# A two-layer attention kernel on one core: in the token tail, the read-out of every odd tile moved up into the round of the even tile before it

## The chip, the core and the metric

The kernel runs on one core of a Trainium2 chip. The metric is the device time of one execution in microseconds, a median over runs. Engines are named as in the profile: PE (TensorE matmuls), PEld (its weight loads), DVE (VectorE), ACT (ScalarE), POOL (GpSimd), SP (the queue that issues most DMAs).

## What is computed

The model has four blocks, A, B, A, B, each with a residual and a layer norm in front. S = 2048 tokens, D = 576 features, 32 heads of 18. A is softmax attention with one shared key and value head; B is linear attention with a feature map of two softmaxes. Cut to what matters here:

```python
# B, per head
phi_q = concat(softmax(q @ w_phi), softmax(-(q @ w_phi)))     # 36 features
kv    = einsum("sf,sd->fd", phi_k, v);  z = phi_k.sum(s)
o     = (phi_q @ kv) / (phi_q @ z + 1e-6)                     # the "read-out"
x     = x + concat_heads(o) @ wo
```

The kernel calls one A and the B behind it a layer, so it has two layers.

## The kernel before, in words

Tokens are worked in 16 tiles of 128. A layer first runs the attention of A (`attend`), with the keys and features of B mixed in. When the last tile's state is known (`leave`, `finish_state`), the state of B stands in `kvb`, and the features of every query tile in DRAM (`phi`). Then comes the tail, on which this case turns. It takes one token tile after another through these steps:

- `load_features` (L718 and L719 on SP): the tile's features from DRAM into `pht`. There are two such buffers, one for even tiles and one for odd ones (`room`).
- the read-out (`read_out`, first part): 22 small matmuls at L826 (the profile records two instructions for each of them, 44 in all) multiply `pht` by `kvb` into two banks of PSUM; each matmul writes only 64 of the output rows, so it uses half of the array's columns. For each bank DVE adds epsilon to the denominators (L833), inverts them (L834) and multiplies (L835); a copy (L836) completes `xo`.
- the transposes (`transposed`): four matmuls at L308 and one at L312 turn `xo` (128 tokens by 640) into two banks. ACT copies the first bank to `xs3` as the high part (L132) and the second (L314), DVE subtracts to get the low part (L135, L317).
- the projection (`project`, L258): 28 matmuls, 14 for each half of the output, with the high and low parts of the weights `wob` (tiles `wahi`, `walo` in this stage). The first two products of a half read the high part of `xs3` alone, the third the low part. DVE adds the result to the residual (L322), and SP stores the tile (L1646 in the last layer, L1648 in the first).
- in the first layer the tail goes on into the next attention (`next_queries`): layer norm of the finished tile (L284 to L291 on DVE, L289 on POOL, L298 and L299 on ACT, into `xn`), five transposes of `xn`, and, for every second tile, the query projection (`project_queries`): 70 matmuls at L465, whose results DVE splits (L494, L498), and a smaller part a round later (L515, L520).

The order is written by generators. Each step ends in `yield STAGE`; `pipelined` starts one tile a round and takes every active tile, the oldest first, to its next `STAGE`; what `project_queries` adds stands last in a round. So a round holds the projection of one tile, the transposes of the next and the read-out of the one after that. A read-out is two rounds after its load, the transposes one round after the read-out, the projection one round after that. What the program writes is then ordered for each engine by the framework's scheduler, which may put a step earlier where it expects a wait. PSUM has seven banks in this stage, given out in turn; `xo` and `xs3` have two buffers each.

Of the kernel before, what the change touches and what calls it, by code (L numbers as in the profile page):

```python
# [52 lines left out]
STAGE = None  # L53
# [9 lines left out]
def kernel(ctx, tc, x_in, wq, wk, wv, wo, wqkv, w_phi, wob, out):  # L63
# [168 lines left out]
    def reload_w4(pool):  # L232
        room_w4(pool)
        for half in range(2):
            nc.sync.dma_start(w4[half].bitcast(F32).rearrange("p k c -> p (k c)"), w4d[half])
# [19 lines left out]
    def project(dst, w, c0, xs, after=None, products=range(len(PRODUCTS)), last=LASTP):  # L255
        for j, n in enumerate(products):
            slot, half, k = PRODUCTS[n]
            T.matmul(dst, xs[:, slot, :], w[half][:, k, c0 : c0 + HALF],  # L258
                     start=(n == 0), stop=(n == last))
            if n == last:  # L260
                if after is not None:
                    after()
                yield -250
            elif j % 2:
                yield 250
# [4 lines left out]
    def bankful(kind, ps, shape=(P, HALF)):  # L270
        yield Kind(kind)
        return ps.tile(list(shape), F32, name="ps")
# [21 lines left out]
    def layer_norm(i, stats, pool, E, tag="xn"):  # L294
        rstd, bias = stats[i]
        xn = pool.tile([P, 5 * P], F32, name=tag)
        if E is A:
            A.activation(xn[:, :D], xres[i], AF.Identity, scale=rstd, bias=bias)  # L298
            A.activation(xn[:, D:], xn[:, 512:D], AF.Copy)  # L299
        else:  # L300
            V.tensor_scalar(xn[:, :D], xres[i], rstd, bias, op0=ALU.mult, op1=ALU.add)
            V.tensor_copy(xn[:, D:], xn[:, 512:D])
        return xn

    def transposed(xn, xs, ps, hi_engine, lo_engine=V):
        pa = ps.tile([P, 4, P], F32, name="ps")
        for k in range(4):
            T.transpose(pa[:, k, :], xn[:, k * P : (k + 1) * P], idf)  # L308
        split(xs[:, 0:4, :], xs[:, 5:9, :], pa, hi_engine, lo_engine)
        yield -440  # L310
        pb = ps.tile([P, P], F32, name="ps")
        T.transpose(pb, xn[:, 512:], idf)  # L312
        if hi_engine is A:
            A.activation(xs[:, 4, :], pb, AF.Copy)  # L314
        else:
            V.tensor_copy(xs[:, 4, :], pb)
        lo_engine.tensor_sub(xs[64:P, 4, :], pb[64:P, :], xs[64:P, 4, :].bitcast(F32))  # L317
        yield -110

    def add_residual(i, b, po):  # L320
        xr = xres[i][:, b * HALF : (b + 1) * HALF]
        V.tensor_add(xr, xr, po)  # L322
# [458 lines left out]
    def advance(job, count=1):  # L781
        while count:
            v = next(job, DONE)
            if v is DONE:
                return
            count -= v is not STAGE and not isinstance(v, Kind) and v < 0
# [31 lines left out]
    def read_out(i, pht, st, sp, ps):  # L818
        xo = sp.tile([P, 5 * P], F32, name="xo")
        xv = xo[:, :D].rearrange("p (h d) -> p h d", d=DH)  # L820
        for g0, g1 in ((0, 8), (8, NKG)):
            pn = ps.tile([P, 8 * NW], F32, name="ps")
            for g in range(g0, g1):
                hs = KG if g < NKG - 1 else 2
                for t0 in (0, 64):
                    T.matmul(pn[t0 : t0 + 64, (g - g0) * NW : (g - g0) * NW + hs * (DH + 1)],  # L826
                             pht[: 2 * DH * hs, g, t0 : t0 + 64],
                             st["kvb"][: 2 * DH * hs, g, : hs * (DH + 1)], start=True, stop=True)
            h0, h1 = g0 * KG, min(g1 * KG, H)
            nv = pn[:, : (h1 - h0) * (DH + 1)].rearrange("p (h e) -> p h e", e=DH + 1)  # L830
            den = small.tile([P, 24], F32, name="den")
            dv = den[:, : h1 - h0]
            V.tensor_scalar(dv, nv[:, :, DH], 1e-6, None, op0=ALU.add)  # L833
            V.reciprocal(dv, dv)  # L834
            V.tensor_mul(xv[:, h0:h1, :], nv[:, :, :DH], dv[:, :, None].to_broadcast([P, h1 - h0, DH]))  # L835
        V.tensor_copy(xo[:, D:], xo[:, 512:D])  # L836
        yield STAGE
        xs = sp.tile([P, 9, P], F32R, name="xs3")
        yield from transposed(xo, xs, ps, A)
        yield STAGE  # L840
        for b in range(2):
            po = yield from bankful("P", ps)
            yield from project(po, st["wob"], b * HALF, xs, lambda: add_residual(i, b, po))
# [544 lines left out]
    for layer in range(LAYERS):  # L1388
        last = layer == LAYERS - 1
        st.update(start_state(bw), added=set(), loaded=set())  # L1390
        with tc.tile_pool(name="a1o", bufs=2) as a1o:
# [166 lines left out]
            def feature_room(name):  # L1558
                return bw.tile([P, H, 2, DH], F32, name=name)
# [26 lines left out]
        with psx, tc.tile_pool(name=f"s{layer + 1}", bufs=2) as sp:  # L1586
            if not last:
                reload_w4(sp)

            def leave():  # L1590
                xn = layer_norm(c, stats, sp, A, "xo")
                advance(second_keys)
                xl = sp.tile([P, 9, P], F32R, name="xs3")
                advance(transposed(xn, xl, ps, A, LOE), 2)
                queued = [queries_in(i, x, feature_room(name), st, ps, spills[layer])
                          for i, x, name in ((KEPT, kept, "featk"), (c - 1, xs, "featq"))]
                advance(queued[0])
                both = sp.tile([P, 9, PW], F32R, name="xsc").bitcast(F32).rearrange("p a b -> p (a b)")
                ek, eq = (both[:, k * 2 * D : (k + 1) * 2 * D].rearrange("p (h s d) -> p h s d", s=2, d=DH)
                          for k in range(2))  # L1600
                last_keys = keys_in(c, xl, ek, st, ps)
                queued.append(queries_in(c, xl, eq, st, ps, spills[layer]))
                advance(last_keys, 2)
                run(load("wob", "a", wob, slice(0, D), engines=(A, V)))
                advance(last_keys, 2)
                if not last:
                    run(load("wq", "b", wq, slice(0, D), engines=(A, G)))
                advance(queued[0])
                advance(last_keys)
                advance(queued[2])  # L1610
                run(finish_state(st, sp, ps))
                advance(queued[2])
                advance(queued[1])
                run(queued[0])
                before = None
                for i in traced(nc)[mark:]:
                    if i.engine == mybir.EngineType.PE:
                        if before is not None:
                            tc.add_manual_dep(i, before, NOSYNC, reason="order")
                        before = i.name  # L1620
                return queued[1:]

            def flips(queued):
                for rounds, job, count in ((1, 0, 1), (3, 0, 3), (2, 1, 3)):
                    for _ in range(rounds):
                        yield STAGE
                    advance(queued[job], count)
                for job in queued:
                    run(job)

            def room(i):
                if i % 2:
                    return sp.tile([P, NKG, P], F32, name="pht", bufs=1)
                return bw.tile([P, NKG, P], F32, name="pht")

            def token_tile(i):
                pht = room(i)
                load_features(pht, spills[layer], i)
                if i not in left:
                    xres[i] = sp.tile([P, D], F32, name="xt", bufs=6)  # L1640
                    nc.sync.dma_start(xres[i], xd[i])
                yield STAGE
                yield STAGE
                yield from read_out(i, pht, st, sp, ps)
                if last:
                    nc.sync.dma_start(out[i * P : (i + 1) * P, :], xres[i])  # L1646
                else:
                    nc.sync.dma_start(xd[i], xres[i])  # L1648
                    yield STAGE
                    yield from next_queries(i, None, layer + 1, st, bw, sp, ps)  # L1650

            order = range(NT)
            st["sp"] = sp
            jobs = [token_tile(i) for i in order]
            for job in jobs[:2]:
                next(job)
            st["late"].append(flips(leave()))
            if last:
                run(pipelined(jobs, st["late"]))
            else:  # L1660
                settle(layer + 1, ps, jobs)
# [27 lines left out]
```

## Time and profile before

| | us |
|---|---|
| median of 3 runs | 2626.08 |
| lowest and highest run | 2624.30, 2628.52 |
| span of the profiled execution (first to last instruction) | 2624.6 |
| first layer's tail, first to last read-out | 1230.2 to 1375.6 |
| second layer's tail, first read-out to the end | 2519.5 to 2624.6 |

The span is that of one profiled execution; the page gives no time for it beside the span, which lies within the three runs, 1.5 us under their median. Over the span PE is busy 99%, ACT 82%, DVE 48%. In a timeline row the columns are start and duration in us, engine, line, operation, tiles (out<-in), shapes and the number of instructions merged, and in brackets how long the engine sat idle before and what ended that.

### The profile page before, as it was taken

Reading aid. Unit: us, or ns where it says so; the run is one execution under the profiler, and the core shown is the slowest. Engines: PE = TensorE matmul, PEld = TensorE weight load, DVE = VectorE, ACT = ScalarE, POOL = GpSimd, SP = SyncE. Lnnn points to the kernel's source line nnn. Section 1 sums busy time; section 2 is a strip of 40 time slices with the busy share of each in tenths; the row PEclk is TensorE's granted clock in tenths of the full one; section 3 lists DMA queues with packets and bytes.
Section 4 is the critical chain, followed back from the end, with each engine's and each line's share of the span. In section 5 each row is a group of like instructions: output and inputs, shape, how many; then the busy total and the mean of one; then the engine's idle time right before and its main releaser. Section 6 shows DMA issues by size and latency. Waiting matters only on the chain. (4 is left out here: it accounts for less than half of the span.)

```text
span 2624.6 us, 55489 instructions
## 1 busy us (share of the span) xinstructions
PE 2585.7 (99%) x22002; PEld 1428.7 (54%) x22002; DVE 1252.3 (48%) x2831; ACT 2163.5 (82%) x2578; POOL 66.0 (3%) x106
## 2 busy tenths in 40 slices
PE   7999999999999999999999999999999999999999
PEld 7634444444444444438996344444444444444598
DVE  7434554444444444427775324444444444444265
ACT  5699899999999999993335999999999999999721
POOL 1000000000000000002000000000000000000010
PEclk9999999999999999999999999999999999999999
DMA  6456352222222222225644222222222222222164
GB/s 194 139 137 185 97 153 59 59 60 57 58 57 61 61 61 61 61 53 179 196 138 131 82 57 57 59 61 56 61 61 61 61 61 61 61 60 57 38 197 145
DMA packets 491632, 232.94 MB, mean 89 GB/s; under 512 B 237734, under 2 KB 458214, under 8 KB 491366
## 3 DMA queue, kind: packets, MB, share of 16 engines
q1 hardware_dynamic: 490326, 227.26, 31.5%
q8 instruction: 175, 2.87, 0.5%
q10 hardware_dynamic: 1040, 2.06, 0.3%
q14 instruction: 91, 0.75, 0.1%
HBM read 130.62 MB, written 96.67 MB: 87 GB/s over the span
## 5 line engine op out<-in xcount | busy, mean ns | idle before, releaser
L1101 ACT ACTIVATE pt<-sc 128x1024 f32<-128x1024 f32 x2032 | 1923.4, 1062 | 146.8 <-PE sc L595 120.1
L595 PE MATMUL sc<-qst,kst 56*128 56x512 f32 x3840 | 687.3, 449 | 1.7 <-ACT pt L1101 1.4
L595 PEld LDWEIGHTS sc<-qst,kst 56*128 56x128 f32 x3840 | 317.0, 184 | 555.2 <-ACT pt L1101 509.1
L875 PE MATMUL acc<-pt,vst 128*32 128x512 f32 x4096 | 510.7, 600 | 0.2 <-DVE vb L660 0.2
L875 PE MATMUL ps<-pt,vst 128*32 128x512 f32 x4048 | 483.4, 600 | 0.0
L875 PEld LDWEIGHTS ps<-pt,vst 128*32 128x32 f32 x4048 | 108.9, 109 | 225.8 <-issue 225.0
L875 PEld LDWEIGHTS acc<-pt,vst 128*32 128x32 f32 x4096 | 98.5, 108 | 201.0 <-issue 189.1
L322 DVE TENSOR_TENSOR xc<-xc,acc 128x288 f32<-128x288 f32 x59 | 26.8, 454 | 326.8 <-PE acc L258 326.8
L629 DVE COPY featq<-ps 128x288 f32<-128x288 f32 x52 | 23.8, 458 | 266.9 <-PE ps L258 266.9
L258 PE MATMUL ps<-wahi,xs 128*128 128x288 f32 x684 | 147.0, 301 | 1.9 <-ACT xs L132 1.9
L258 PE MATMUL ps<-wchi,xs 128*128 128x288 f32 x576 | 127.4, 306 | 0.0
L258 PE MATMUL acc<-wdhi,on 128*128 128x288 f32 x531 | 117.4, 306 | 0.0
L258 PEld LDWEIGHTS ps<-wahi,xs 128*128 128x128 f32 x684 | 111.8, 188 | 5.6 <-ACT xs L132 2.6
L258 PE MATMUL ps<-walo,xs 128*128 128x288 f32 x380 | 111.2, 295 | 0.0
L465 PE MATMUL ps<-xsc,wbhi 128*128 128x256 f32 x576 | 107.8, 286 | 0.7 <-ACT xsc L132 0.7
L132 ACT ACTIVATE xs<-ps 128x512 fp32r<-128x512 f32 x36 | 21.4, 595 | 102.6 <-PE ps L308 102.6
L258 PE MATMUL acc<-wahi,xs 128*128 128x288 f32 x468 | 103.8, 307 | 1.3 <-DVE turned L1009 1.3
L258 PEld LDWEIGHTS ps<-wchi,xs 128*128 128x128 f32 x576 | 94.0, 188 | 16.1 <-issue 15.7
L258 PEld LDWEIGHTS acc<-wdhi,on 128*128 128x128 f32 x531 | 86.5, 187 | 21.2 <-issue 21.2
L629 DVE COPY featk<-acc 128x288 f32<-128x288 f32 x52 | 23.8, 457 | 153.2 <-PE acc L258 153.2
L258 PE MATMUL ps<-wclo,xs 128*128 128x288 f32 x320 | 94.2, 294 | 0.0
L465 PEld LDWEIGHTS ps<-xsc,wbhi 128*128 128x128 f32 x576 | 91.4, 193 | 1.5 <-ACT xsc L132 1.1
(263 smaller groups left out, 3075.9 us busy)
## 6 DMA issues: line engine op xcount, KB each, us to landing
qst<-qd SPq DMA_DIRECT2D x360, 72.0 KB
od<-parts SPq DMA_DIRECT2D x512, 36.0 KB
pht<-phi SPq DMA_DIRECT2D x32, 540.0 KB
qd<-pc SPq DMA_DIRECT2D x64, 256.0 KB
on<-od SPq DMA_DIRECT2D x60, 256.0 KB
phi<-pht SPq DMA_DIRECT2D x104, 144.0 KB
xd<-xc SPq DMA_DIRECT2D x33, 288.0 KB
flipped<-pht SPq DMA_DIRECT2D x112, 72.0 KB
```

The lines of the kernel that those rows point to most:

```text
L132: A.activation(dst_hi, src, AF.Copy)
L258: T.matmul(dst, xs[:, slot, :], w[half][:, k, c0 : c0 + HALF], start=(n == 0), stop=(n == last))
L322: V.tensor_add(xr, xr, po)
L465: T.matmul(po, lhs, xsc[:, slot, :], start=(n == 0), stop=(n == LASTP))
L595: T.matmul(sc, kst[head_rows(h), t * P : (t + 1) * P], q[head_rows(h), h // 2, :], start=True, stop=True)
L629: V.tensor_copy(e[:, hs, 0, :], src)
L875: T.matmul(acc[32 * j : 32 * j + 32, :], vst[:, t, :], pts[j], start=first, stop=last)
L1101: A.activation(pt, sc, AF.Exp, scale=SCALE)
```

## The change

In `read_out` the wait between an odd tile's read-out and its transposes becomes two rounds instead of one; in `token_tile` the wait between an odd tile's load and its read-out becomes one round instead of two. So the read-out of tile 2n+1 stands in the round of the read-out of tile 2n, right behind it, and all its later steps keep their rounds. Rounds alternate: one with two read-outs, one with none. The tail of both layers is written by these lines.

```diff
@@ read_out
         V.tensor_copy(xo[:, D:], xo[:, 512:D])
-        yield STAGE
+        for _ in range(1 + i % 2):
+            yield STAGE
         xs = sp.tile([P, 9, P], F32R, name="xs3")
         yield from transposed(xo, xs, ps, A)
@@ token_tile
-                yield STAGE
-                yield STAGE
+                for _ in range(1 if i % 2 else 2):
+                    yield STAGE
                 yield from read_out(i, pht, st, sp, ps)
```

Three places show what the scheduler makes of it. The numbers behind the tiles' names tell buffers apart.

PE, second layer, tiles 10 to 12, before: `xo_30704` is the read-out of tile 10, `pht_30654` the features of tile 11, `xs3_30776` the transposed tile 10.

```order
L308 MATMUL ps_30777<-idf_82,xo_30704 128x128 x4
L312 MATMUL ps_30784<-idf_82,xo_30704 128x128
L826 MATMUL ps_30789<-kvb_29726,pht_30654 64x57 x16
L826 MATMUL ps_30810<-kvb_29726,pht_30654 64x57 x4
L826 MATMUL ps_30810<-kvb_29726,pht_30654 64x38 x2
L258 MATMUL ps_30825<-wahi_29596,xs3_30776 128x288
L258 MATMUL ps_30825<-walo_29597,xs3_30776 128x288
L258 MATMUL ps_30825<-wahi_29596,xs3_30776 128x288 x2
```

Tile 11's read-out stands between tile 10's transposes and its projection. The same place with the change: `xo_30704` and `xs3_30810` belong to tile 10, `xo_30738` to tile 11.

```order
L308 MATMUL ps_30811<-idf_82,xo_30704 128x128 x4
L312 MATMUL ps_30818<-idf_82,xo_30704 128x128
L258 MATMUL ps_30825<-wahi_29596,xs3_30810 128x288
L258 MATMUL ps_30825<-walo_29597,xs3_30810 128x288
L258 MATMUL ps_30841<-wahi_29596,xs3_30810 128x288
L258 MATMUL ps_30841<-walo_29597,xs3_30810 128x288
L308 MATMUL ps_30859<-idf_82,xo_30738 128x128 x2
L258 MATMUL ps_30825<-wahi_29596,xs3_30810 128x288 x2
```

The read-out that stood between a tile's transposes and its projection is gone from this round; the projection begins with the first two products of both halves, and two of the next tile's transposes come behind these four matmuls. The other round of the pair, with the features of tiles 12 and 13:

```order
L308 MATMUL ps_30859<-idf_82,xo_30738 128x128 x2
L312 MATMUL ps_30866<-idf_82,xo_30738 128x128
L826 MATMUL ps_30871<-kvb_29726,pht_30772 64x57 x16
L826 MATMUL ps_30892<-kvb_29726,pht_30772 64x57 x4
L826 MATMUL ps_30892<-kvb_29726,pht_30772 64x38 x2
L826 MATMUL ps_30905<-kvb_29726,pht_30822 64x57 x16
L826 MATMUL ps_30926<-kvb_29726,pht_30822 64x57 x4
L826 MATMUL ps_30926<-kvb_29726,pht_30822 64x38 x2
L258 MATMUL ps_30941<-wahi_29596,xs3_30858 128x288
```

The read-out of tile 13 has moved up to that of tile 12, between the transposes of tile 11 and its projection.

DVE, first layer, around the read-outs of tiles 2 and 3, before: `den_14671`, `den_14682` and `xo_14653` are tile 2's read-out, `mv1_14731` to `lnb1_14740` tile 1's layer norm.

```order
L833 TENSOR_SCALAR den_14671<-ps_14654 128x24
L285 BN_AGGR mv1_14731<-bnst_14732 128x2
L834 RECIPROCAL den_14671<-den_14671 128x24
L833 TENSOR_SCALAR den_14682<-ps_14675 128x8
L835 TENSOR_TENSOR xo_14653<-ps_14654,den_14671 128x432
L834 RECIPROCAL den_14682<-den_14682 128x8
L287 TENSOR_SCALAR var1_14736<-mv1_14731 128x1
L835 TENSOR_TENSOR xo_14653<-ps_14675,den_14682 128x144
L291 SCALAR_TENSOR_TENSOR lnb1_14740<-mv1_14731,rstd1_14738 128x1
L836 COPY xo_14653<-xo_14653 128x64
```

The layer norm's steps are mixed with tile 2's read-out here. With the change tile 3's read-out is `den_14705`, `den_14716` and `xo_14687`, and tile 1's layer norm `mv1_14765` to `lnb1_14774`.

```order
L835 TENSOR_TENSOR xo_14653<-ps_14675,den_14682 128x144
L833 TENSOR_SCALAR den_14705<-ps_14688 128x24
L836 COPY xo_14653<-xo_14653 128x64
L833 TENSOR_SCALAR den_14716<-ps_14709 128x8
L834 RECIPROCAL den_14705<-den_14705 128x24
L834 RECIPROCAL den_14716<-den_14716 128x8
L835 TENSOR_TENSOR xo_14687<-ps_14688,den_14705 128x432
L835 TENSOR_TENSOR xo_14687<-ps_14709,den_14716 128x144
L285 BN_AGGR mv1_14765<-bnst_14766 128x2
L836 COPY xo_14687<-xo_14687 128x64
L287 TENSOR_SCALAR var1_14770<-mv1_14765 128x1
L291 SCALAR_TENSOR_TENSOR lnb1_14774<-mv1_14765,rstd1_14772 128x1
```

The layer norm's last steps on DVE, from L285 on, have moved behind the whole read-out of tile 3.

PE, first layer, behind the transposes of tile 6 (`xo_15200`), before, with the features of tile 7 (`pht_15015`) and the layer norm of tile 4 (`xn_15277`):

```order
L308 MATMUL ps_15314<-idf_82,xo_15200 128x128 x4
L312 MATMUL ps_15321<-idf_82,xo_15200 128x128
L826 MATMUL ps_15326<-kvb_14358,pht_15015 64x57 x16
L826 MATMUL ps_15347<-kvb_14358,pht_15015 64x57 x4
L826 MATMUL ps_15347<-kvb_14358,pht_15015 64x38 x2
L308 MATMUL ps_15365<-idf_82,xn_15277 128x128 x4
L312 MATMUL ps_15372<-idf_82,xn_15277 128x128
L258 MATMUL ps_15390<-wahi_14216,xs3_15313 128x288
```

Tile 7's read-out stands between the two groups of transposes. With the change, the layer norm of tile 4 being `xn_15311`:

```order
L308 MATMUL ps_15348<-idf_82,xo_15200 128x128 x4
L312 MATMUL ps_15355<-idf_82,xo_15200 128x128
L308 MATMUL ps_15365<-idf_82,xn_15311 128x128 x4
L312 MATMUL ps_15372<-idf_82,xn_15311 128x128
L258 MATMUL ps_15390<-wahi_14216,xs3_15347 128x288
```

Here the layer norm's transposes follow those of tile 6 with nothing between. Apart from the two tails the order of the engines' instructions is the same.

## The prediction

> **What bounds the kernel now.** I read the page first, then the busy time by windows, then the timeline of both tails.
>
> ```profile
> PE 2585.7 (99%) x22002; PEld 1428.7 (54%) x22002; DVE 1252.3 (48%) x2831; ACT 2163.5 (82%) x2578; POOL 66.0 (3%) x106
> 1262.00:1400.00 138.00, 138.00 (x1457) 132.58 (x1456) 100.27 (x315) 50.11 (x122) 7.03 (x13) 1.00 0.51 154
> 1420.00:1440.00 20.00, 19.02 (x114) 5.54 (x118) 6.40 (x15) 18.01 (x21) 0.00 (x0) 0.85 0.45 135
> 2556.00:2604.00 48.00, 48.00 (x625) 46.28 (x625) 28.16 (x89) 6.12 (x16) 0.00 (x0) 1.00 0.60 187
> 2604.00:2624.60 20.60, 16.33 (x186) 15.27 (x184) 9.19 (x27) 2.30 (x6) 0.00 (x0) 0.99 0.15 58
> ```
>
> A window's row gives its length, the busy time of PE, PEld, DVE, ACT and POOL, the granted clock, the DMA share and GB/s. Over most of both tails PE has no idle time at all (138.00 of 138.00 us, 48.00 of 48.00), so the change is worth what it does to PE's own sequence: the steps between one kind of matmul and the next, and any wait that it lays bare. One round of the second layer's tail, and the kernel's last transposes, where no read-out follows:
>
> ```profile
> 2609.98 0.27 PE L312 MATMUL ps<-idf,xo 128*128 128x128 f32 x1
> 2610.18 1.48 PE L826 MATMUL ps<-kvb,pht 108*64 108x57 f32 x44
> 2611.59 0.40 PE L258 MATMUL ps<-wahi,xs 128*128 128x288 f32 x1
> 2611.83 0.29 PE L258 MATMUL ps<-walo,xs 128*128 128x288 f32 x1
> ...
> 2615.87 0.27 PE L312 MATMUL ps<-idf,xo 128*128 128x128 f32 x1
> 2616.07 0.60 ACT L132 ACTIVATE xs<-ps 128x512 fp32r<-128x512 f32 x1 [5.13 <-PE ps L308]
> 2616.70 0.69 DVE L135 TENSOR_TENSOR xs<-ps,xs 128x512 fp32r<-128x512 f32 x1 [0.61 <-ACT xs L132]
> 2616.72 0.40 PE L258 MATMUL ps<-wahi,xs 128*128 128x288 f32 x1 [0.58 <-ACT xs L132]
> 2616.96 0.30 PE L258 MATMUL ps<-walo,xs 128*128 128x288 f32 x1
> ```
>
> The read-out has a second task that the code doesn't name: it fills the time in which ACT copies the transposed tile. Where it is missing, PE marks 0.58 us idle for that copy.
>
> **What the change saves: changes of kind.** For a read-out alone between transposes and a projection, I go from the start of L312 to the start of the second L258, since the first L258 starts early and the second late: 2611.83 - 2609.98 = 1.85 us. The same step with no read-out and no wait, and the read-out matmul's duration:
>
> ```profile
> 1193.78 0.27 PE L312 MATMUL ps<-idf,xn 128*128 128x128 f32 x1
> 1193.81 0.38 PE L258 MATMUL ps<-wbhi,xs 128*128 128x288 f32 x1
> 1194.03 0.30 PE L258 MATMUL ps<-wblo,xs 128*128 128x288 f32 x1
> ...
> L826 PE MATMUL ps<-kvb,pht x1408: 206/222/265, 1230.3 to 2611.4; 108*64 108x57 f32 x160, 72*64 72x38 f32 x16
> ```
>
> That is 0.25 us, so a lone read-out costs 1.60 us. One that follows another needs no change of kind: its last matmul starts at 2610.18 + 1.48 - 0.22 = 2611.44, so 43 steps take 1.26 us, and 44 take 1.29. It saves 0.31 us; no row shows two read-outs in a row, so the bounds are a saving of nothing (1.60) and this. The Trainium skill ("TensorE: Matmul & The Clock Gate", Back-to-back issue gap) gives small matmuls a floor of about 25 ns from start to start; by it the second read-out would cost an estimated 1.10 us and the sum below would be some 3 us lower, but this trace's own step is 29 ns and decides.
>
> **What the change costs: the cover.** The order shows the second layer's even tiles with their projection right behind their transposes, eight times. From L312 to the second L258 this takes 2616.96 - 2615.87 = 1.09 us, so 0.84 more than 0.25. The products with the low part, which wait for L135 (2616.70), need no price: two or three of the next tile's transposes now stand ahead of them. Lower bound: the 0.58 that PE marks as idle. One small stall goes, as two read-outs now stand between tile 0's `xo` and its transposes:
>
> ```profile
> 2523.82 0.30 PE L312 MATMUL ps<-idf,xo 128*128 128x128 f32 x1 [0.31 <-DVE xo L836]
> ```
>
> Second layer: 8 x (0.84 - 0.31) - 0.31 = +3.9 us.
>
> In the first layer the order leaves other work there. For tiles 4 and 14 it is 70 query matmuls, for 8, 10 and 12 it is L515, L520 and the layer norm's transposes: no wait. Tile 0 has nothing, but there PE comes to a stop that DMA sets:
>
> ```profile
> 1243.63 0.29 PE L826 MATMUL ps<-kvb,pht 108*64 108x57 f32 x2 [1.46 <-DMA pht<-phi]
> ```
>
> This load of tile 2 keeps its place on SP, and +0.84 - 0.31 - 0.31 fits into 1.46, so I take nothing. Two places remain, tiles 2 and 6, where the layer norm's transposes stand behind the tile's own and now wait for ACT:
>
> ```profile
> 1248.64 1.41 PE L696 MATMUL ps<-idf,featq 128*108 128x128 f32 x11
> 1249.89 0.60 PE L308 MATMUL ps<-idf,xn 128*128 128x128 f32 x4
> 1250.44 0.60 PE L308 MATMUL ps<-idf,xo 128*128 128x128 f32 x4
> ...
> 1285.06 0.54 POOL L289 TENSOR_TENSOR rstd<-var,neghalf 128x1 f32<-128x1 f32 x1 [16.49 <-DVE var L287]
> 1285.63 0.16 DVE L291 SCALAR_TENSOR_TENSOR lnb<-mv,rstd 128x1 f32<-128x1 f32 x1 [0.16 <-POOL rstd L289]
> 1285.88 0.87 ACT L298 ACTIVATE xn<-xt,lnb,rstd 128x576 f32<-128x576 f32 x1 [2.65 <-issue]
> 1286.54 0.27 PE L312 MATMUL ps<-idf,xo 128*128 128x128 f32 x1
> 1286.77 0.26 ACT L299 ACTIVATE xn<-xn 128x64 f32<-128x64 f32 x1
> 1286.94 0.58 ACT L132 ACTIVATE xs<-ps 128x512 fp32r<-128x512 f32 x1
> 1287.29 0.21 DVE L285 BATCH_NORM_AGGREGATE mv<-bnst 128x2 f32<-128x12 f32 x1
> 1288.60 0.26 DVE L833 TENSOR_SCALAR den<-ps 128x24 f32<-128x24 f32 x2
> 1288.88 0.36 DVE L834 RECIPROCAL den<-den 128x24 f32<-128x24 f32 x2
> 1289.22 0.82 DVE L835 TENSOR_TENSOR xo<-ps,den 128x432 f32<-128x432 f32 x2
> ```
>
> *Tile 2.* Its read-out ends on PE at 1248.64 (L696 starts). PE would go on with tile 3's (1.29), L696 (1249.89 - 1248.64 = 1.25), and three groups of transposes (1250.44 - 1249.89 = 0.55 each), to the projection at 1252.85. DVE works on the read-out from 1288.60 to 1290.04, 1.44 us: tile 2's till 1250.0; then, with a copy of some 0.2 between, tile 3's till 1251.7; only then L285 (0.21) and, with a copy and L287 at some 0.3, the variance at 1252.2. POOL to L291 takes 0.57, L291 to L298 0.25, L298 to the next 0.89: 1253.9. In the changed order ACT copies `xs3` (0.6) before L299 (0.26): 1254.8, and the last of these transposes needs L299. The wait is 2.0 us; were DVE free of tile 3's read-out (1.6), it would be 0.4.
>
> *Tile 6.* L298 ends about when L312 does, 1286.77. Then the copy and L299 end at 1287.6, where PE would be done with these transposes at 1286.54 + 0.55 = 1287.1: 0.5 us. Tile 7's read-out, a round sooner on DVE, pushes the layer norm back by up to 0.5: I take 1.0.
>
> The saving: three of the pairs 2-3 to 14-15 save 0.31. In the other four the lone read-out was followed by L515, itself another kind, so that only one of two changes goes: half, 0.15. Together 1.5. First layer: -1.5 + 2.0 + 1.0 = +1.5 us.
>
> **Queues.** SP issues two loads of `pht` back to back in place of one a round. The buffers come free with the read-outs, as before, and the next pair is a pair of rounds away, so an odd tile's load has 10 us where the first ones of the second layer have about 9:
>
> ```profile
> 2522.70 0.33 SPq L718 DMA_DIRECT2D pht<-phi  x1
> ...
> 2531.36 0.56 PE L826 MATMUL ps<-kvb,pht 108*64 108x57 f32 x10
> ```
>
> The stores and residual loads behind them on SP come later, which nobody on PE waits for: cost nothing; if a load were late, its price is in the third rival. Two read-outs hold four PSUM banks; bank by bank, the next user of each of the seven stands a round or nearly one behind, and DVE needs 1.44 us of it for each read-out: nothing.
>
> **The sum.** 3.9 + 1.5 = 5.4 us on the profiled span of 2624.6, so 2630.0; the median of the runs lies 1.5 us above that span: 2626.08 + 5.4 = **2631.5 us**, 0.21% slower. About 0.2% (5.25 us) is also what a measurement of this kernel can tell from no change; a value under 2631.3 counts as the same.
>
> **The rivals.**
>
> *The layer norm's waits don't come (not slower).* Place: tiles 2 and 6 of the first layer. If DVE is free in time, they cost 0.4 and 0.5 instead of 3.0, and the time is 2631.5 - 2.1 = 2629.4. It decides from the point where both together stay under 2.8 us. For it: the scheduler chose that order. Against: the sum of L833 to L836 for tile 3 alone is 1.6 us. Chance 0.20.
>
> *The cover suffices everywhere.* The moved transposes would have to hide the copy. Then only savings stay: 8 x 0.31 + 0.31 in the second layer, 1.5 in the first: 2626.1 - 4.3 = 2621.8; with the cheaper second read-out of the skill 2618.8. Against: they stand behind the first four projection matmuls, which themselves wait; the last tile of the trace shows the 0.58. Chance 0.06, a third of it below 2620.8.
>
> *The odd tile's features come late.* The first layer's wait of 1.46 on this very load shows that it can happen; twice more it gives 2631.5 + 2.9 = 2634.4. Against: the 60% DMA share in the second tail. Chance 0.10.
>
> *The clock drops.* In 1420 to 1440, where PE's idle time is 0.98 us in short waits, the granted clock is 0.85. Over the 98 us of the second tail before its last tile that would add 98 x (1 / 0.85 - 1) = 17 us: 2649. The Trainium skill ("TensorE: Matmul & The Clock Gate", A second HAM failure mode) says that frequent micro-idles between groups of matmuls can make the gate swing. Against: the last window holds the 0.58 wait at a clock of 0.99. Chance 0.02.
>
> That the change doesn't do what it says is excluded by the order.
>
> **How the numbers follow.** The forecast keeps 0.62. Its own bounds: low, 0.58 for each of the eight waits (8 x 0.27 - 0.31 = 1.9) with 0.4 and 0.5 in the first layer (-0.6), +1.3, so 2627.4; high, half the saving lost on the second read-outs (16 x 0.15 = 2.4) and 0.6 more at the layer norm, +8.4, so 2634.5. This holds the first rival and the third at its price, so I give 2627.4 to 2634.5. The forecast lies just above the bound; of its 0.62 I put 0.39 above, as waits that I have not seen lengthen more readily than they shorten. Slower: 0.39 + 0.10 + 0.02 = 0.51. Same: 0.23 + 0.20 + 0.04 = 0.47. Faster: 0.02.
>
> **What would show it.** Right: in the second tail PE idle about 0.58 before L258 with ACT `xs` L132 as releaser, eight or nine times instead of twice; 88 L826 in a row in under 2.8 us; two rounds there taking 12.3 us instead of 11.8; in the first layer one wait of about 2 us for `xn` L298 or L299 after tile 3's read-out. Wrong: no such idle time, a second L826 group starting late for DMA, or a clock below 1.00 in the tails.

## The result, and the profile with the change

Over 21 runs of each kernel the median went from 2626.3 us to 2630.5 us; the ratio is 1.0015 with a 95% interval of 1.0009 to 1.0021. So the change costs 4.2 us, 0.16%: the forecast was 5.4, and the outcome lies just inside the 0.2% that was called no change. Of the forecast's three classes "same" came, with a chance of 0.47, and not "slower", with 0.51, though the interval leaves out 1.

The profiled span grew by only 1.7 us, from 2624.6 to 2626.3. That is no measure of the change: the first read-out matmul started at 1230.27 us before and at 1227.62 now, and nothing ahead of it was changed. The tails have to be compared by themselves. In the tables of this part, the first tail goes from the first L826 to the first matmul of the next attention (L595), the second from its first L826 to the last L258; all are starts in the timelines of PE.

| | first tail | second tail |
|---|---|---|
| before | 1230.27 to 1376.67: 146.40 | 2519.54 to 2620.62: 101.08 |
| with the change | 1227.62 to 1374.46: 146.83 | 2517.49 to 2622.32: 104.83 |
| difference | +0.43 | +3.75 |

The two differences make 4.18 us, which is the 4.2 of the medians. That they agree so closely is chance: in time the interval of the ratio is 2.4 to 5.5 us, and the first tail of one program differs by 2 us and more from execution to execution (table below). The forecast had +1.5 and +3.9.

The second tail first: what PE waited for there (us in total, number of times, longest), the only row of that view for this stretch.

```profile
PE ps L258 <- ACT xs L132: 6.0, 10, 0.8
```

Ten projections wait for ACT's copy of the transposed tile: those of the eight even tiles, and of tiles 1 and 15, which waited before too:

```profile
PE ps L258 <- ACT xs L132: 1.2, 2, 0.6
```

The timeline of PE around tiles 4 and 5, and the start of tile 6:

```profile
2551.00 0.27 PE L312 MATMUL ps<-idf,xo 128*128 128x128 f32 x1
2551.85 0.40 PE L258 MATMUL ps<-wahi,xs 128*128 128x288 f32 x1 [0.58 <-ACT xs L132]
2552.09 0.30 PE L258 MATMUL ps<-walo,xs 128*128 128x288 f32 x1
...
2556.13 0.27 PE L312 MATMUL ps<-idf,xo 128*128 128x128 f32 x1
2556.33 2.76 PE L826 MATMUL ps<-kvb,pht 108*64 108x57 f32 x88
2559.03 0.40 PE L258 MATMUL ps<-wahi,xs 128*128 128x288 f32 x1
2559.26 0.29 PE L258 MATMUL ps<-walo,xs 128*128 128x288 f32 x1
...
2564.15 0.40 PE L258 MATMUL ps<-wahi,xs 128*128 128x288 f32 x1 [0.58 <-ACT xs L132]
2564.39 0.30 PE L258 MATMUL ps<-walo,xs 128*128 128x288 f32 x1
```

Tile 4 has nothing between its transposes and its projection and waits (0.58 marked as idle); tile 5 has two read-outs there, 88 recorded instructions without a gap, and does not. From tile 4's projection to tile 6's, one pair of rounds takes 2564.39 - 2552.09 = 12.30 us; before, the same two matmuls start 11.78 us apart:

```profile
2552.91 0.29 PE L258 MATMUL ps<-walo,xs 128*128 128x288 f32 x1
...
2564.69 0.29 PE L258 MATMUL ps<-walo,xs 128*128 128x288 f32 x1
```

The waits of PE in the first tail:

```profile
PE ps L826 <- DMA pht<-phi: 1.5, 1, 1.5
PE ps L258 <- ACT xs L132: 1.2, 2, 0.6
PE ps L308 <- ACT xn L298: 1.1, 1, 1.1
```

The last row is new: transposes of a layer norm that was late, at tile 2. The DMA row is the wait for tile 2's features, 1.5 us as before, and one of the two for L132 is tile 0's, new too.

### The profile page after: what moved, and what is told of

Its sections match the earlier page's. It is cut to its first block, busy times and chain, and to the rows that moved or that the text cites. A ratio compares the mean times of both kernels' runs of the same rounds, so it can differ in the third digit from the quotient of the medians.

```text
span 2626.3 us, 55495 instructions
## 1 busy us (share of the span) xinstructions
PE 2581.0 (98%) x22002; PEld 1425.7 (54%) x22002; DVE 1250.7 (48%) x2831; ACT 2163.1 (82%) x2578; POOL 66.0 (3%) x106
## 3 DMA queue, kind: packets, MB, share of 16 engines
q10 hardware_dynamic: 1040, 2.06, 0.3%
## 5 line engine op out<-in xcount | busy, mean ns | idle before, releaser
L595 PE MATMUL sc<-qst,kst 56*128 56x512 f32 x3840 | 687.5, 450 | 1.7 <-ACT pt L1102 1.4
L595 PEld LDWEIGHTS sc<-qst,kst 56*128 56x128 f32 x3840 | 317.3, 184 | 554.8 <-ACT pt L1102 508.8
L258 PE MATMUL ps<-wahi,xs 128*128 128x288 f32 x684 | 147.8, 302 | 7.2 <-ACT xs L132 7.2
L258 PE MATMUL ps<-wchi,xs 128*128 128x288 f32 x576 | 127.4, 307 | 0.0
L258 PEld LDWEIGHTS ps<-wahi,xs 128*128 128x128 f32 x684 | 111.8, 188 | 12.3 <-ACT xs L132 10.1
L258 PE MATMUL acc<-wdhi,on 128*128 128x288 f32 x531 | 117.5, 307 | 0.0
L258 PE MATMUL ps<-walo,xs 128*128 128x288 f32 x380 | 111.3, 296 | 0.0
L132 ACT ACTIVATE xs<-ps 128x512 fp32r<-128x512 f32 x36 | 21.5, 596 | 103.3 <-PE ps L308 103.3
L258 PE MATMUL acc<-wahi,xs 128*128 128x288 f32 x468 | 103.8, 308 | 1.3 <-DVE turned L1010 1.3
L258 PEld LDWEIGHTS ps<-wchi,xs 128*128 128x128 f32 x576 | 94.1, 188 | 16.2 <-issue 16.0
L258 PEld LDWEIGHTS acc<-wdhi,on 128*128 128x128 f32 x531 | 86.6, 188 | 21.2 <-issue 21.2
L258 PE MATMUL ps<-wclo,xs 128*128 128x288 f32 x320 | 94.2, 295 | 0.0
```

The source lines that it names most:

```text
L132: A.activation(dst_hi, src, AF.Copy)
L595: T.matmul(sc, kst[head_rows(h), t * P : (t + 1) * P], q[head_rows(h), h // 2, :], start=True, stop=True)
```

## The experiments

The theory was that of the prediction: read-outs back to back save about 0.3 us a pair, and moving them lays bare the copy of every even tile, plus two waits for the layer norm in the first layer. The general rival was that read-outs in pairs cost time by themselves. Times of an experiment are medians, beside runs of the kernel before on the same chip; a ratio can differ by up to 0.0004 from the quotient of the medians. In the kernels whose `transposed` was edited, line numbers behind it are three higher (L829 is the read-out, L317 ACT's second copy), and the last transpose, L312, is L313 or L315. All the tails:

| kernel | first tail | wait for tile 2's features in it | second tail | ratio to before (95%) |
|---|---|---|---|---|
| before | 146.40 | 1.46 | 101.08 | |
| change | 146.83 | 1.47 | 104.83 | 1.0015 (1.0009 to 1.0021) |
| e1, second layer only | 148.18 | 1.71 | 104.84 | 1.0014 (1.0005 to 1.0023) |
| e2, first layer only | 146.99 | 1.59 | 101.08 | 1.0002 (0.9993 to 1.0011) |
| e3, pairs all through | 147.35 | 3.10 | 96.41 | 0.9992 (0.9983 to 1.0001) |
| e4, change with fill | 146.38 | 1.03 | 106.12 | 1.0019 (1.0010 to 1.0029) |
| e5, before with fill | 148.52 | 2.06 | 107.17 | 1.0028 (1.0017 to 1.0039) |
| e6, copy in halves | 150.18 | 1.96 | 103.23 | 1.0009 (0.9999 to 1.0019) |
| e7, two pairs skipped | 145.54 | 0.78 | 104.87 | 1.0012 (1.0002 to 1.0022) |
| e8, e3 in the second layer | 146.24 | 1.32 | 96.69 | 0.9979 (0.9970 to 0.9988) |
| e9, e3 from tile 4 on | 150.73 | 1.58 | 96.79 | 0.9985 (0.9976 to 0.9994) |

The second tail repeats to 0.04 us where its program is the same (104.83, 104.84, 104.87; 101.08 twice). The first does not: the wait for tile 2's features differs from execution to execution, and after some of the longer ones PE runs slowly for a few us (last section). So the first tail is also read from the end of that wait to the next attention: before 1243.63 to 1376.67, 133.04 us; the change 133.44 (1241.02 to 1374.46).

**e1 and e2: one layer at a time.**

```diff
-                for _ in range(1 if i % 2 else 2):
+                paired = i % 2 and last            # e2: i % 2 and not last
+                for _ in range(1 if paired else 2):
                     yield STAGE
```

with two rounds behind the read-out where `paired` holds.

> The change in the second layer's tail alone. Theory: the loss is the copy that ACT makes of each even tile, which PE now waits out because no read-out stands there; it is a matter of the second layer. From the first read-out to the last projection matmul of the second tail the profile of before has 101.08 us and that of the changed kernel 104.83: this run 104.8 in the second tail and 146.4 in the first (before 146.40), and +3.75 us in all (ratio 1.0014). Rival (the loss comes with each pair of read-outs, wherever it is): half of the 4.2 us of the whole change, +2.1 us.

> The change in the first layer's tail alone. Theory: the savings at the changes of kind (about 1.3 us) and the two waits for the layer norm at tiles 2 and 6 (1.5 and 0.45 us) nearly cancel: first tail 146.8 (before 146.40), second tail 101.1, +0.4 us in all (ratio 1.0002). Rival (the loss comes with each pair): +2.1 us.

e1 took 2629.79 us against 2625.93, +3.9; e2 2626.16, +0.2. Their second tails are those of the change and of before. e2's first tail, from the end of the wait on, is 133.46 us, the change's 133.44; that of e1, whose first layer is the kernel before, is 1.5 longer than before's by the slow matmuls told of below, which the expectation did not know. The loss is nearly all in the second layer, where the theory has it, and is not spread over the pairs. The rival's +2.1 us, a ratio of 1.0008, lies inside both intervals, so the times alone do not rule it out; the tails do.

**e3: pairs all the way.** Transposes of both tiles, then the next two read-outs, then both projections, in both layers (edits to the change):

```diff
-        for _ in range(1 + i % 2):
+        for _ in range(2):
             yield STAGE
         xs = sp.tile([P, 9, P], F32R, name="xs3")
         yield from transposed(xo, xs, ps, A)
-        yield STAGE
+        for _ in range(1 + i % 2):
+            yield STAGE
```

> Read-outs in pairs as in the change, but both tiles' transposes stand together ahead of the next two read-outs, and both projections behind them: every copy is covered again, in both layers. Theory: per pair the second read-out costs 1.28 instead of 1.60 us, the second group of transposes needs no change of kind (about as much again less the step between projections): 0.33 us less than before per pair; with eight pairs, tile 0's wait for xo (0.31) and the last tile's wait cut by the other tile's transposes (about 0.5), the second tail is 101.08 - 3.2 = 97.9 us. First tail: six or seven pairs, less 1 to 2 us if no wait for the layer norm appears. In all -4 to -5 us (ratio 0.998). Rival (read-outs back to back themselves cost time, by PSUM banks or loads that come late): second tail at or above 101.1, no gain.

The timeline of PE in its second tail, without most of the projections' matmuls:

```profile
2537.15 0.60 PE L308 MATMUL ps<-idf,xo 128*128 128x128 f32 x4
2537.58 0.27 PE L312 MATMUL ps<-idf,xo 128*128 128x128 f32 x1
2537.69 0.60 PE L308 MATMUL ps<-idf,xo 128*128 128x128 f32 x4
2538.13 0.27 PE L312 MATMUL ps<-idf,xo 128*128 128x128 f32 x1
2538.33 2.76 PE L826 MATMUL ps<-kvb,pht 108*64 108x57 f32 x88
```

Read-outs still stand in pairs, and PE marks no wait in this tail at all. It takes 96.41 us, 4.7 less than before (3.2 expected; in the steady rounds a pair takes 11.45 instead of 11.78 us, the 0.33 of the theory; most of the rest came at the last tile, the second matmul of whose projection starts 3.86 us behind tile 14's instead of 5.13, and before's waits of 0.31 us for tile 0's `xo` and of 0.64 ahead of tile 1's projection are gone). So pairs of read-outs do not cost time; a missing cover does. In time only 2.1 us of it was left (2623.81): the first tail was 0.95 longer, with a wait of 3.1 us for tile 2's features, and from the last L258 to the last instruction it took 5.4 us instead of 4.0. That late end did not come again in e8 and e9.

**e4 and e5: useless work in the place of the wait.** Behind the transposes of every even tile of the second layer, seven more into a part of the bank that nothing reads:

```diff
         T.transpose(pb, xn[:, 512:], idf)
+        for n in range(fill):                      # 7
+            T.transpose(pf[:, 1 + n % 3, :], xn[:, 512:], idf)
```

> The changed kernel with useless work added in the second layer: behind the transposes of each even tile PE does seven more transposes into a part of the bank that nobody reads. Seven steps of 0.109 us are 0.76 us, a little less than the 0.84 us by which the copy holds up the projection. Theory: they fit into the wait, so the second tail stays at 104.8 us and the marked idle time of PE ahead of L258 falls from about 0.6 to under 0.1 at each even tile. Rival (PE does not really wait there, the time goes elsewhere): 8 x 0.76 more, 110.9 us.

> The same seven transposes per even tile added to the kernel before, where the odd tile's read-out already covers the copy. Theory: nothing hides them, 8 x 0.76 = 6.1 us more: second tail 107.2 us, ratio 1.0023. Rival (there is room on PE in both kernels): 101.1.

Tile 6 in e4, PE and ACT:

```profile
2565.86 0.27 PE L313 MATMUL ps<-idf,xo 128*128 128x128 f32 x1
2565.96 0.93 PE L315 MATMUL ps<-idf,xo 128*128 128x128 f32 x7
2566.05 0.60 ACT L132 ACTIVATE xs<-ps 128x512 fp32r<-128x512 f32 x1 [6.40 <-PE ps L308]
...
2566.71 0.40 PE L258 MATMUL ps<-wahi,xs 128*128 128x288 f32 x1
...
2566.95 0.29 PE L258 MATMUL ps<-walo,xs 128*128 128x288 f32 x1
```

The projection starts when the copy ends, as without the fill: 2566.95 - 2565.86 = 1.09 us from the one transpose to the second projection matmul, the same 1.09 as in the change (2552.09 - 2551.00), and no idle time is marked. In the kernel before, the same 56 transposes lengthen the second tail by 107.17 - 101.08 = 6.09 us, all of their 6.1 (its time rose by 8.0 us, with an interval of 4.5 to 10.2, in a run whose first tail was 2.1 us longer). In the changed one they add 1.29, not nothing, or 0.16 for each pair: two of the next tile's transposes, which stood behind the projection's fourth matmul (the second fence of the order, ahead of the prediction), stand behind the whole projection in e4's order. In their old place they filled a second wait, that for the low part. In e4 the fifth matmul starts at 2567.43, 0.22 us behind the fourth instead of the usual 0.13, just when DVE's L135 is done (2567.38). From the fourth matmul to the next one with `walo` it takes 0.63 us in the change, the two transposes included, and 0.59 in e4, which spends 0.22 on them later: 0.18 us in this pair. That the same work costs 6.09 us in the one kernel and 1.29 in the other shows the wait.

**e6: the copy in halves.** ACT's copy and DVE's subtraction for the even tiles of the second layer in two steps of 256 columns.

```diff
-        split(xs[:, 0:4, :], xs[:, 5:9, :], pa, hi_engine, lo_engine)
+        step = 2 if halves else 4                  # halves: even tiles, second layer
+        for k in range(0, 4, step):
+            split(xs[:, k : k + step, :], xs[:, 5 + k : 5 + k + step, :], pa[:, k : k + step, :],
+                  hi_engine, lo_engine)
```

> The changed kernel with ACT's copy of the even tiles' first bank, and DVE's subtraction, made in two halves of 256 columns in the second layer. The kernel's other ACT copies of 256 columns take 0.38 us where 512 take 0.60. Theory: the projection waits for the first half alone, so each of the eight waits falls by 0.22 us, or by up to 0.44 if the first half can start behind two transposes: second tail between 101.4 and 103.1 us instead of 104.83. Rival (the wait is for something else than the copy's length): 104.8.

```profile
2556.35 0.27 PE L315 MATMUL ps<-idf,xo 128*128 128x128 f32 x1
2556.55 0.38 ACT L132 ACTIVATE xs<-ps 128x256 fp32r<-128x256 f32 x1 [3.42 <-PE ps L308]
...
2556.99 0.40 PE L258 MATMUL ps<-wahi,xs 128*128 128x288 f32 x1 [0.36 <-ACT xs L132]
2557.23 0.29 PE L258 MATMUL ps<-walo,xs 128*128 128x288 f32 x1
```

The wait falls from 0.58 to 0.36 us, by the 0.22 that the copy is shorter, and the second tail by 1.6 us to 103.23, 0.1 above the range given: the copy starts behind all the transposes (2556.55, 0.20 behind the start of the last), not behind two of them. So the length of this copy sets the wait.

**e7: without the pairs 2-3 and 6-7 of the first layer** (`i % 2 and (last or i not in (3, 7))`).

> The change without the pairs 2-3 and 6-7 of the first layer. Theory: the two waits for the layer norm (1.5 us at tile 2, 0.45 at tile 6) go, and with them the two pairs' savings of about 0.3 us each and the 0.26 by which tile 2's projection had become shorter: first tail 146.83 - 1.95 + 0.9 = 145.8 us, second tail 104.8. Rival (these waits come with any pair whose tile is followed by the layer norm): they show up at other tiles, first tail 146.8 or more.

No wait for `xn` is left in the first tail, so these waits belong to those two pairs. The tail took 145.54 us, 145.8 expected, but partly by a short wait for tile 2's features. From the end of that wait it is 132.85 us, 0.59 less than with the change instead of about 1.0: a new wait of 0.45 us for tile 4's features stands in it.

**e8 and e9: e3's order where the first layer does not spoil it.**

```diff
+                through = last                     # e9: last or i >= 4
```

with e3's rounds where `through` holds, and the rounds of before elsewhere.

> The order of e3 (both transposes, both read-outs, both projections) in the second layer alone, the first layer as in the kernel before. Theory: the second tail is 96.4 us again (101.08 before), and the first is that of before, with the wait for tile 2's features at its 1.5 us or so where e3 had 3.1 and slower matmuls behind it. If the end is as in e3 (5.4 us from the last projection matmul to the last instruction, 3.9 before): -3.2 us, ratio 0.9988; if that was chance: -4.7, 0.9982. Rival (e3's little gain in time means that the saving in the second tail is lost elsewhere in it): no gain, 1.000 as in e3's interval.

> The order of e3 in the second layer and from tile 4 on in the first, whose tiles 0 to 3 keep the order of before, since the wait for tile 2's features stood there. Theory: second tail 96.4 us; first tail five or six pairs at 0.33 us less each, 146.4 - 1.8 = 144.6 us; in all -5 us with the later end of e3 (ratio 0.998), -6.5 without. Rival (in the first layer the layer norm's waits eat the saving, as at tile 2 of the change): first tail 146.4 or more and a total like e8's.

e8 took 2621.63 us against 2626.09: ratio 0.9979 (0.9970 to 0.9988), faster than both kernels. Its second tail is 96.69 us, 4.39 under before's, and the time is 4.5 less. PE marks no wait in it, and from the last L258 to the end it takes 4.0 us as before. The rival falls. e9 took 2622.52 (0.9985): the saving in the first layer did not come. From the end of its wait the first tail took 137.25 us; about 2.8 of the 4.2 above before's are slow matmuls behind the wait (from its end to the second matmul of tile 2's projection 12.41 us, in e8 9.59). That leaves 1.4 us more than before where 1.8 less were expected, and the new waits that the profile shows, 0.9 us for a tile's features and 0.5 and 0.2 that it puts down to `xo`, are half of that. The other half stays open. So e9's rival has the outcome right, a first tail over 146.4 and a total like e8's, but its cause is not shown: the profile puts no wait of this tail down to the layer norm's L298.

## Why the prediction was right, and where it was off

The second layer came as worked out. **The second read-out:** from L312 (2556.13) to the second L258 (2559.26) it is 3.13 us, and 1.85 with one read-out, so the second costs 1.28; the forecast had 1.29. The saving against 1.60 is real, and e3 and e8 collect it. **The cover:** 1.09 us from L312 to the second L258, 0.84 above the 0.25 without a wait, as taken from the kernel's last tile. A pair of rounds costs 12.30 - 11.78 = 0.52 us (forecast 0.84 - 0.31 = 0.53). The 0.31 for tile 0's `xo` went. **Tile 0 of the first layer** costs nothing: from the first read-out to the end of the wait for tile 2's features it is 13.36 us before and 13.40 with the change. That these are so near is chance, as the load sets them (12.7 to 14.0 in the other runs), but PE has time to spare there.

The first layer was over-priced, by 1.1 of the 1.2 us between forecast and result. The step that failed is the size of the layer norm's waits, 2.0 us at tile 2 and 1.0 at tile 6; the mechanism is there. Tile 2, after (PE, DVE, ACT):

```profile
1247.35 1.41 PE L696 MATMUL ps<-idf,featq 128*108 128x128 f32 x11
...
1248.70 0.20 DVE L285 BATCH_NORM_AGGREGATE mv<-bnst 128x2 f32<-128x12 f32 x1
...
1249.58 0.27 PE L312 MATMUL ps<-idf,xo 128*128 128x128 f32 x1
...
1250.06 0.89 ACT L298 ACTIVATE xn<-xt,lnb,rstd 128x576 f32<-128x576 f32 x1
...
1251.00 0.66 PE L308 MATMUL ps<-idf,xn 128*128 128x128 f32 x4 [1.14 <-ACT xn L298]
...
1251.30 0.28 ACT L299 ACTIVATE xn<-xn 128x64 f32<-128x64 f32 x1
...
1251.63 0.33 PE L312 MATMUL ps<-idf,xn 128*128 128x128 f32 x1
```

Without a wait the last transpose (1251.63) would stand five steps of 0.11 us behind the one at 1249.58, at 1250.13: the wait is 1.5 us, not 2.0. The order is the one that was read off, L285 behind tile 3's whole read-out on DVE; but L285 starts 1248.70 - 1247.35 = 1.35 us behind the last read-out matmul, where the forecast had 1251.7 - 1249.93 = 1.77. I had put DVE's steps end to end by the busy time of merged rows, and added the copy; in the trace the steps overlap, and from the start of tile 3's L833 (1247.33) to L285 it is 1.37 us with the copy among them. Tile 6:

```profile
1285.37 0.87 ACT L298 ACTIVATE xn<-xt,lnb,rstd 128x576 f32<-128x576 f32 x1 [2.73 <-issue]
...
1285.94 0.27 PE L312 MATMUL ps<-idf,xo 128*128 128x128 f32 x1
...
1286.64 0.25 ACT L299 ACTIVATE xn<-xn 128x64 f32<-128x64 f32 x1
...
1286.94 0.33 PE L312 MATMUL ps<-idf,xn 128*128 128x128 f32 x1
```

Here the last transpose starts at 1286.94 where 1285.94 + 0.55 = 1286.49 was possible: 0.45 us. That is the part without the "0.5" by which tile 7's read-out was to push the layer norm back; there was hardly a push, since L298 ends 0.30 us behind the start of L312, 0.21 before. Together 1.95 us instead of 3.0, under the 2.8 that the first rival named as its point: the time came out on its side of the bound, at +4.2 us between the forecast's +5.4 and its +3.3. One gain was not foreseen: tile 2's 28 projection matmuls took 3.82 us up to what follows them instead of 4.08: before, 0.29 us lie between the second and the third of them (1253.23 and 1253.52) where otherwise 0.13 do, probably for the low part of `xs3`, which now is ready by then. With 1.95 - 0.26 and a net 0.40, 1.3 us are left for the savings in this layer, where 1.5 were taken.

Of the other rivals, the cover did not suffice, and no odd tile's features were late in the second layer. The clock stayed up in the second tail, with its ten waits of 0.58 to 0.77 us (columns: window, length, busy time of PE, PEld, DVE, ACT, POOL, granted clock, DMA share, GB/s):

```profile
2519.00:2627.00 108.00, 97.59 (x1224) 93.03 (x1219) 59.42 (x187) 15.84 (x41) 4.67 (x4) 1.00 0.50 157
```

The clock rival had misread its 0.85 for 1420 to 1440 as the effect of the short waits in that window. It is the mean of a half clock up to 1426.15 and a full one behind, and the half clock began at 1419.32, behind 1.58 us of idle time in the 3.41 us ahead of it (last section).

## What to carry to other kernels

On an engine that is never idle, ask of every step what it hides before it is moved: the read-out's price was 1.60 us, but 0.84 of it was paid by a wait that it covered, so grouping read-outs for a saving of 0.31 lost 0.52 a pair. The saving can be had when the covered steps are grouped as well, so that one cover serves both tiles (e8). Waits in a chain of small steps on another engine are better taken from starts in a trace than from sums of busy times.

## What the runs showed of the hardware that was not expected

A wait of PE of under 2 us can halve its clock for 3.4 or 6.8 us, and whether it does depends on where it falls. It is the wait for tile 2's features in the first layer. In e2 and in e9 it is as long to 0.01 us:

```profile
1243.23 0.56 PE L826 MATMUL ps<-kvb,pht 108*64 108x57 f32 x10 [1.59 <-DMA pht<-phi]
```

```profile
1242.79 0.43 PE L826 MATMUL ps<-kvb,pht 108*64 108x57 f32 x2 [1.58 <-DMA pht<-phi]
```

The clock fell in e9 alone. In all eleven traces the granted clock changes only at points of a grid of 3.413 us: in e9 at 1242.39, 1249.22, 1423.30 and 1430.13 us, which are 2, 51 and 2 steps apart; in e2 at 1419.58 and 1426.41, so that 1242.09, 52 steps ahead, is a point of its grid. The steps around the wait, e2 and then e9 (columns as above):

```profile
1238.68:1242.09 3.41, 2.32 (x16) 1.84 (x14) 3.23 (x8) 0.77 (x2) 1.57 (x2) 1.00 0.86 256
1242.09:1245.50 3.41, 2.27 (x23) 2.21 (x24) 2.67 (x7) 0.00 (x1) 2.79 (x3) 1.00 0.62 206
```

```profile
1238.98:1242.39 3.41, 1.59 (x11) 1.12 (x10) 3.05 (x8) 0.77 (x2) 1.02 (x2) 1.00 0.85 261
1242.39:1245.81 3.42, 3.02 (x13) 2.95 (x14) 1.94 (x4) 0.73 (x1) 2.64 (x3) 0.50 0.52 157
1245.81:1249.22 3.41, 3.41 (x17) 3.13 (x16) 0.92 (x2) 0.39 (x2) 0.00 (x0) 0.50 0.28 87
```

In e2 a point of the grid cuts the wait in two, and PE is idle for 1.09 and 1.14 us of the two steps. In e9 most of the wait and the 0.64 us for a copy ahead of it fall into one step, 1.82 us of it are idle, and the next two run at half clock. In the first tails of all the traces the step ahead of a drop had 1.71 (e1), 1.82 (e9), 1.91 (e5), 2.25 (e6) or 3.05 us (e3) of idle time, and no other step more than 1.52 (change): the bound lies near half a step. It is not sharp by the profile's idle time, since elsewhere 1.58 us were enough (before, ahead of 1419.32) and 1.83 were not (e4, 214.61 to 218.02). The half clock lasted one step where PE was busy all through it (e1, e3, e5), and two where 0.35 or 0.40 us of the first were idle (e6, e9).

From the end of the wait to the next attention the same program takes 133.04 us in before and e8, and 134.58 and 134.57 in e1 and e5, where the clock fell; with the change's first layer it takes 133.44 to 133.46 in the change, e2 and e4, and 136.30 in e6. The Trainium skill ("TensorE: Matmul & The Clock Gate", HAM oscillation — how this bites in real kernels) has as its abstract rule that PE should have no idle gaps over about 3.4 us; here gaps of half that were enough. This place, whose load the change does not move, makes the largest difference between single executions of the first tail.
